# Matmuls that read their moving operand by turns from its two halves, in an attention and MLP kernel

## The chip, the cores and the metric

The kernel runs on one core of a Trainium2 chip. The metric is the device time of one launch in microseconds (us), the median of several runs. Work on the host before and after the launch is not in it.

## The reference

```python
scores = scale * np.matmul(z, z.transpose(0, 2, 1))   # scale = 1 / S
attn = np.maximum(scores, 0.0) ** 2
out = np.matmul(attn, v)
x = (u * out).reshape(B * S, D)
...
h = x @ w_in
relu6 = np.clip(h + 3.0, 0.0, 6.0)
g = h * relu6 / 6.0
return (g @ w_out).astype(np.float32)
```

B = 4 batches, S = 3008 tokens, D = 256, 64 columns of z, and 2048 columns between the two projections. Everything is float32, w_in and w_out come as float64.

## The kernel before, in words

Tokens stand along the free dimension of the tiles. Each batch is cut into six chunks of query tokens, five of 512 columns and one of 448 (`width`, L508), and into twelve pairs of key blocks of 128. A matmul takes a stationary operand of 128x128 and streams a moving operand of up to 512 columns into a PSUM bank. All of them go through one helper, `mm` (L74), so every matmul of the profile has line 75, and they are told apart by their tiles.

To keep precision, a float32 number is split into a high and a low part of type float32r, and a product is made of three: high by high, high by low, low by high.

- `scores` (L416) makes a pair of score blocks with two matmuls for each block (tile s, from zx and zy); ScalarE applies relu, ScalarE and VectorE square, and the result is split into ah and al. Part of the score blocks is not computed: they are the transposes of blocks made before, which come back from DRAM (`keep` L340, `fetch_pair` L325, `turn` L366).
- `av` (L513) sums attention times v into o: per chunk, pair and half of D six matmuls, four with ah as the moving operand (against vl and vh) and two with al; the last pair of a chunk has five. `first_av` (L496) is the same for the very first pair.
- `times_u` (L544) multiplies o by u, which `load_u` (L537) brought in as a block of two chunks, and `split_x` (L552) cuts the block of 1024 or 960 tokens into a left and a right half of 512 or 480 columns, forms the sums of the second operand of a seven-product scheme for 2x2 blocks, and splits them into xh and xl.
- `group` (L671) makes for one block and one eighth of the 2048 columns the seven products, three matmuls each (tile m; `product`, L684), and the gate; results are split into gh and gl.
- `downs_of` (L607) has the second projection (tile y): six matmuls for each half of the tokens and of D, in `one` (L634) and, for the last eighth of the last block, `last_one` (L611). `store_y` (L651) scales y and writes it out.

The order of all this is written out by hand in the loop of L845: pair by pair, the score matmuls of the pair after next, the attention sums of this pair, and from pair 33 on pieces of `group` and `down` between them; the instructions run in that order on each engine. The program has 688 score matmuls, 3408 of attention, 2016 of the first projection, 2304 of the second, and ten on zeros at the start (`warm_up`, L818).

Of the kernel before, what the change touches and what calls it, by code (L numbers as in the profile page):

```python
# [13 lines left out]
B, S, D, DQK, DFF = 4, 3008, 256, 64, 2048  # L14
NT = B * S
P = 128
CH = 512
NCH = 6
# [4 lines left out]
NFP = NF // 2  # L23
# [18 lines left out]
def relu2_attention_then_hswish_mlp(  # L42
# [30 lines left out]

    def mm(out, lhsT, rhs, start, stop, part=False):  # L74
        nc.tensor.matmul(out, lhsT=lhsT, rhs=rhs, start=start, stop=stop, skip_group_check=part)  # L75

    def sub(out, a, b):
        nc.vector.tensor_tensor(out=out, in0=a, in1=b, op=ALU.subtract)  # L78
# [4 lines left out]
    def split(hi, lo, raw, rounded=False):  # L83
        if not rounded:
            nc.scalar.copy(out=hi, in_=raw)  # L85
        sub(lo, raw, f(hi))
# [409 lines left out]
    def first_av():  # L496

        for d in range(2):
            ot[d] = ps.tile([P, CH], F32, tag=f"o{d}", name=f"o{d}")
        ah, al = at[0, 0, 0]  # L500
        vh, vl = vt[0, 0]
        for k, (a, w, r) in enumerate(
            [(ah, w, r) for r in range(2) for w in (vl, vh)] + [(al, vh, r) for r in range(2)]
        ):
            for d in range(2):
                mm(ot[d], w[:, r, d * P:(d + 1) * P], a[:, r], k == 0, False)

    def width(c):  # L508
        return CH if c < NCH - 1 else S - CH * (NCH - 1)

    ot = {}

    def av(b, c, p, d):  # L513

        n = width(c)
        first = p == pairs_of(b, c)[0]
        if first:
            home = f"y0{d}" if (b, c) == (0, 1) else f"o{d}"
            ot[d] = ps.tile([P, CH], F32, tag=home, name=f"o{d}")
        o = ot[d][:, :n]  # L520
        ah, al = at[b, c, p]
        vh, vl = vt[b, p]
        dd = slice(d * P, d * P + P)
        last = p == NPAIR - 1
        passes = [(w, ah, r) for r in range(2) for w in (vl, vh)]
        passes += [(vh, al, r) for r in range(1 if last else 2)]
        for k, (w, a, r) in enumerate(passes):
            mm(o, w[:, r, dd], a[:, r, :n], first and k == 0, last and k == len(passes) - 1)

    raw_x = {}  # L530

    def tokens(i):

        b, c = divmod(i, NCH // 2)
        return b * S + 2 * c * CH, width(2 * c) + width(2 * c + 1)
# [14 lines left out]
    xt = {}  # L550
# [56 lines left out]
    def downs_of(i, q, gs):  # L607

        n = tokens(i)[1] // 2

        def last_one(h, e):  # L611
            o = yt_t[h, e]
            gh, gl = gs[h]
            ee = slice(e * P, e * P + P)
            w = wo[i, q]
            y = rpool.tile([P, 2, CH], F32, tag="r", name="y")[:, e, :n]
            order = (1, 0) if h else (0, 1)
            for r in order:
                mm(o[:, :n], w[:, 1, r, ee], gh[:, r, :n], False, False)
                mm(o[:, :n], w[:, 0, r, ee], gh[:, r, :n], False, False)  # L620
                mm(o[:, :n], w[:, 0, r, ee], gl[:, r, :n], False, r == order[1])
            if e:
                nc.vector.tensor_scalar(
                    out=y, in0=o[:, :n], scalar1=1.0 / 6.0, scalar2=None, op0=ALU.mult
                )
            else:
                nc.scalar.activation(out=y, in_=o[:, :n], func=AF.Copy, scale=1.0 / 6.0)
            t0 = tokens(i)[0] + h * n
            nc.sync.dma_start(out=yt[e * P:(e + 1) * P, t0:t0 + n], in_=y)

        if (i, q) == (NPR - 1, NFP - 1):
            return [(h, e, last_one) for h in range(2) for e in range(2)]

        def one(h, e):  # L634
            if q == 0:
                yt_t[h, e] = ps.tile([P, CH], F32, tag=f"y{h}{e}", name=f"y{h}{e}")
            o = yt_t[h, e][:, :n]
            gh, gl = gs[h]
            ee = slice(e * P, e * P + P)
            w = wo[i, q]  # L640
            for r in range(2):
                mm(o, w[:, 1, r, ee], gh[:, r, :n], q == 0 and r == 0, False)
                mm(o, w[:, 0, r, ee], gh[:, r, :n], False, False)
            for r in range(2):
                mm(o, w[:, 0, r, ee], gl[:, r, :n], False, q == NFP - 1 and r == 1)
            if q == NFP - 1 and e == 1:
                store_y(i, h)

        return [(h, e, one) for h in range(2) for e in range(2)]
# [21 lines left out]
    def group(m, x_bank="x", y_bank="y"):  # L671


        i, q = divmod(m, NFP)
        n = tokens(i)[1] // 2
        if m + 1 < NPR * NFP:
            wi[m + 1] = fetch_w("in", (m + 1) % NFP)
        wo[i, q] = fetch_w("out", q)
        w = wi.pop(m)

        def bank(tag):
            return ps.tile([P, CH], F32, tag=tag, name="m")[:, :n]

        def product(o, a, b, start, stop):  # L684
            xh, xl = xt[i][b]
            mm(o, w[:, 1, a], xh, start, False, True)
            mm(o, w[:, 0, a], xl, False, False, True)
            mm(o, w[:, 0, a], xh, False, stop, True)

        def temp(name):  # L690
            return rpool.tile([P, 2, CH], F32, tag="r", name=name)[:, :, :n]

        def gate(out, h):
            nc.vector.scalar_tensor_tensor(  # L694
                out=out, in0=out, scalar=6.0, in1=h, op0=ALU.min, op1=ALU.mult
            )

        def g_tiles(h):
            gh = gpool.tile([P, 2, CH], F32R, tag=f"gh{h}", name=f"gh{h}")
            gl = gpool.tile([P, 2, CH], F32R, tag=f"gl{h}", name=f"gl{h}")  # L700
            return gh[:, :, :n], gl[:, :, :n]

        end = m == NPR * NFP - 1

        def by_halves(g, r, t):
            split(g[0][:, r], g[1][:, r], t[:, r])

        c21 = bank(x_bank)
        product(c21, A11, B11, True, False)
        ra = temp("ra")  # L710
        nc.scalar.copy(out=ra[:, 1], in_=c21)
        yield
        y = bank(y_bank)
        product(y, A12, B21, True, True)
        add(ra[:, 1], ra[:, 1], y)
        yield
        product(c21, S2, T2, False, False)
        hb = temp("hb") if x_bank == "o0" else hpool.tile([P, 2, CH], F32, tag="hb", name="hb")[:, :, :n]
        nc.scalar.copy(out=hb[:, 0], in_=c21)
        nc.scalar.activation(out=ra[:, 0], in_=ra[:, 1], func=AF.Relu, bias=three)  # L720
        late.append(lambda: gate(ra[:, 0], ra[:, 1]))
        yield
        product(c21, S3, T3, False, False)
        nc.scalar.copy(out=hb[:, 1], in_=c21)
        yield
        y = bank(y_bank)
        product(y, S1, T1, True, False)
        add(hb[:, 1], hb[:, 1], y)
        if end:
            ga, gb, rb = g_tiles(0), g_tiles(1), temp("rb")  # L730
            by_halves(ga, 0, ra)
            nc.scalar.activation(out=rb[:, 1], in_=hb[:, 1], func=AF.Relu, bias=three)
        yield
        product(c21, A22, T4, False, True)
        nc.scalar.activation(out=ra[:, 1], in_=c21, func=AF.Relu, bias=three)  # L735
        gate(ra[:, 1], c21)
        yield
        product(y, S4, B22, False, True)
        add(hb[:, 0], hb[:, 0], y)
        if end:  # L740
            nc.scalar.copy(out=ga[0][:, 1], in_=ra[:, 1])
            nc.scalar.activation(out=rb[:, 0], in_=hb[:, 0], func=AF.Relu, bias=three)
            sub(ga[1][:, 1], ra[:, 1], f(ga[0][:, 1]))
            gate(rb[:, 1], hb[:, 1])
            yield
            nc.scalar.copy(out=gb[0][:, 1], in_=rb[:, 1])
            gate(rb[:, 0], hb[:, 0])
            sub(gb[1][:, 1], rb[:, 1], f(gb[0][:, 1]))
            by_halves(gb, 0, rb)
            downs.extend(downs_of(i, q, (ga, gb)))  # L750
            yield
            return
        ga = g_tiles(0)
        nc.scalar.copy(out=ga[0], in_=ra)  # L754
        yield
        sub(ga[1], ra, f(ga[0]))
        rb = temp("rb")
        nc.scalar.activation(out=rb, in_=hb, func=AF.Relu, bias=three)
        yield
        gate(rb, hb)  # L760
        gb = []

        def rest():
            gb.extend(g_tiles(1))
            split(*gb, rb)

        late.append(rest)
        downs.extend(downs_of(i, q, (ga, gb)))
        yield
# [56 lines left out]
    with tc.manual_schedule():  # L826
# [152 lines left out]
        last = (NPR - 1) * NFP - 1  # L979
# [31 lines left out]
_INS = ["zz", "v", "ut", "w_in", "w_out"]  # L1011


# [30 lines left out]
```

## Time and profile before

| | |
|---|---|
| median of 3 runs | 1907.8 us (1907.55 to 1912.01) |
| profiled execution, span | 1906.0 us |
| around the span (median less span) | 1.8 us |
| PE busy | 1892.2 us, 99%, 8426 matmuls |
| PE weight loads busy | 1574.6 us, 83%, 8426 |
| DVE busy | 1510.6 us, 79%, 1783 instructions |
| ACT busy | 1199.6 us, 63%, 1640 instructions |
| DMA moved | 329.50 MB, mean 173 GB/s |

The profiled execution is known by its span, from the first to the last instruction of the core. PE is TensorE, PEld its weight loads (which overlap its matmuls), DVE VectorE, ACT ScalarE, SP the engine that issues most DMAs. Ends of matmuls are modelled, so that neighbours overlap in the rows; the starts tell their pace.

### The profile page before, as it was taken

The page shows a single profiled execution, that of the slowest core. Times are in us where ns is not written, and L with a number is a line of the kernel's source. Part 1 is how long each engine was busy: PE and PEld are TensorE (multiplying, and loading weights), DVE is VectorE, ACT ScalarE, POOL GpSimd, SP SyncE. Part 2 cuts the span into 40 slices and gives each one's busy share as a digit, 9 for nine tenths or more (in the row PEclk, how much of TensorE's full clock was granted, in tenths as well). Part 3 has the DMA queues.
Part 4 walks back from the last instruction along what each step waited for, and adds up shares of the span by engine and source line. Part 5 has one row for each costly group of instructions (what it writes and reads, how often), then busy time and mean ns, then how long its engine had stood idle before and what let it go on. Part 6 is the DMA issues. An engine that isn't in the chain of part 4 may idle for free.

```text
span 1906.0 us, 23339 instructions
## 1 busy us (share of the span) xinstructions
PE 1892.2 (99%) x8426; PEld 1574.6 (83%) x8426; DVE 1510.6 (79%) x1783; ACT 1199.6 (63%) x1640; POOL 55.5 (3%) x90
## 2 busy tenths in 40 slices
PE   9999999999999999999999999999999999999999
PEld 7877788888888888888888888888888888888887
DVE  8899988878678778887767877888876786787766
ACT  7896656766556556576655655667665565564565
POOL 1000000100000000010000000001000000000000
PEclk9999999999999999999999999999999999999999
DMA  8878978665645675955655666595555567576343
GB/s 232 220 230 219 256 185 219 155 186 184 173 130 163 152 168 120 246 161 174 190 147 138 178 165 162 136 236 156 148 188 137 167 175 171 132 165 161 110 157 121
DMA packets 440307, 329.50 MB, mean 173 GB/s; under 512 B 278656, under 2 KB 397440, under 8 KB 440192
## 3 DMA queue, kind: packets, MB, share of 16 engines
q1 hardware_dynamic: 432672, 304.16, 59.1%
q0 software_dynamic: 7520, 23.86, 4.4%
q8 instruction: 66, 1.08, 0.2%
q14 instruction: 49, 0.40, 0.1%
HBM read 241.70 MB, written 86.25 MB: 172 GB/s over the span
## 4 chain that ended last, share of the span: by engine, by line
PE 66%; issue 23%; DVE 6%; ACT 2%; DMA 2%; SPq 0%; POOL 0%; DVEq 0%; POOLq 0%; ACTq 0%
PE o L75 26%; PE y L75 19%; PE m L75 16%; PE s L75 5%; DVE al L78 1%; DMA l<-d 1%; DVE gl L78 1%; DVE rb L694 0%; DMA dwout<-wh 0%; DVE r L452 0%; DVE rm L373 0%; DMA zraw<-in_zz_dram 0%; DVE xl L78 0%; SPq L334 0%; DVE vl L78 0%
## 5 line engine op out<-in xcount | busy, mean ns | idle before, releaser
L75 PE MATMUL m<-xh,wi 128*128 128x512 f32 (+1 forms) x1344 | 488.6, 387 | 2.8 <-DVE hb L81 1.2
L75 PE MATMUL o<-ah,vl 128*128 128x512 f32 (+1 forms) x1152 | 445.4, 387 | 2.4 <-DVE vl L78 1.2
L75 PE MATMUL o<-ah,vh 128*128 128x512 f32 (+1 forms) x1152 | 444.4, 386 | 0.0
L75 PE MATMUL y<-gh,wo 128*128 128x512 f32 (+1 forms) x1536 | 407.0, 386 | 1.2 <-DMA wo<-dwout 0.7
L75 PE MATMUL o<-al,vh 128*128 128x512 f32 (+1 forms) x1104 | 339.8, 386 | 0.5 <-DVE al L78 0.5
L75 PEld LDWEIGHTS y<-gh,wo 128*128 128x128 f32 x1536 | 288.0, 188 | 57.2 <-ACT gh L754 1.9
L75 PEld LDWEIGHTS m<-xh,wi 128*128 128x128 f32 x1344 | 252.2, 188 | 56.8 <-DVE hb L81 3.6
L75 PE MATMUL m<-xl,wi 128*128 128x512 f32 (+1 forms) x672 | 259.5, 386 | 0.0
L75 PEld LDWEIGHTS o<-ah,vl 128*128 128x128 f32 x1152 | 216.1, 188 | 48.2 <-DVE u L548 3.2
L75 PEld LDWEIGHTS o<-ah,vh 128*128 128x128 f32 x1152 | 216.4, 188 | 42.0
L75 PEld LDWEIGHTS o<-al,vh 128*128 128x128 f32 x1104 | 207.2, 188 | 40.4 <-DVE al L78 0.9
L433 ACT ACTIVATE rt<-s 128x512 f32<-128x512 f32 (+1 forms) x310 | 180.2, 595 | 90.2 <-PE s L75 84.3
L75 PE MATMUL y<-gl,wo 128*128 128x512 f32 (+1 forms) x768 | 234.7, 386 | 0.1
L452 DVE TENSOR_TENSOR r<-rt 128x1024 f32<-128x1024 f32 (+2 forms) x128 | 147.7, 1154 | 99.3 <-ACT rt L433 99.1
L81 DVE TENSOR_TENSOR hb<-hb,m 128x512 f32<-128x512 f32 (+1 forms) x192 | 129.0, 672 | 83.9 <-PE m L75 75.6
L735 ACT ACTIVATE ra<-m,three 128x512 f32<-128x512 f32 (+1 forms) x96 | 65.3, 681 | 198.9 <-PE m L75 195.4
L78 DVE TENSOR_TENSOR al<-r,ah 128x1024 fp32r<-128x1024 f32 (+3 forms) x147 | 164.6, 1120 | 7.1 <-ACT r L450 5.2
L75 PEld LDWEIGHTS y<-gl,wo 128*128 128x128 f32 x768 | 143.9, 188 | 28.5 <-DVE gl L78 0.9
L459 ACT ACTIVATE ah<-rt 128x1024 fp32r<-128x1024 f32 (+1 forms) x155 | 163.8, 1057 | 4.9
L78 DVE TENSOR_TENSOR gl<-rb,gh 128x1024 fp32r<-128x1024 f32 (+2 forms) x97 | 115.4, 1190 | 63.8 <-ACT gh L85 63.2
L78 DVE TENSOR_TENSOR al<-rm,ah 128x1024 fp32r<-128x1024 f32 (+1 forms) x132 | 155.4, 1177 | 1.3 <-ACT ah L400 0.9
L373 DVE STREAM_TRANSPOSE rm<-l 128x1024 f32<-128x1024 f32 (+2 forms) x132 | 149.6, 1133 | 4.1 <-DMA l<-d 4.1
(87 smaller groups left out, 2178.1 us busy)
## 6 DMA issues: line engine op xcount, KB each, us to landing
wi<-dwin SPq DMA_DIRECT2D x96, 896.0 KB, 5.4
d<-r SPq DMA_DIRECT2D x212, 256.0 KB, 3.2
wo<-dwout SPq DMA_DIRECT2D x96, 512.0 KB, 6.1
l<-d SPq DMA_DIRECT2D x304, 128.0 KB, 3.8
l<-d SPq DMA_DIRECT2D x160, 112.0 KB, 4.9
vraw<-in_v_dram POOLq DMA_DIRECT2D x33, 256.0 KB, 3.4
u<-in_ut_dram SPq DMA_DIRECT2D x8, 1024.0 KB, 5.3
out_dram<-y SPq DMA_DIRECT2D x16, 512.0 KB, 5.3
```

Of the source, the lines that this page charges most:

```text
L75: nc.tensor.matmul(out, lhsT=lhsT, rhs=rhs, start=start, stop=stop, skip_group_check=part)
L78: nc.vector.tensor_tensor(out=out, in0=a, in1=b, op=ALU.subtract)
L81: nc.vector.tensor_tensor(out=out, in0=a, in1=b, op=ALU.add)
L373: nc.vector.transpose(out=rn[:, :, :n].rearrange("p r (k e) -> p r k e", e=32), in_=t[:, :n // 32].rearrange("p k (r e) -> p r k e", r=2),)
L433: nc.scalar.activation(out=rn[:, r], in_=s[:, :n], func=AF.Relu, scale=1.0 / S)
L452: nc.vector.tensor_tensor(out=to, in0=of, in1=of, op=ALU.mult)
L459: nc.scalar.activation(out=hn, in_=rn, func=AF.Square)
L735: nc.scalar.activation(out=ra[:, 1], in_=c21, func=AF.Relu, bias=three)
```

## The change

A new helper `paired` gives a moving operand of n columns as a pattern in which the column index runs through two halves by turns: 0, n/2, 1, n/2 + 1, ... The moving operands of `av`, `first_av`, `group` and `downs_of` are read through it; those of `scores` and `warm_up` are not. A matmul's output is still written side by side, so the tokens of o, m and y stand in another order than those of the operand read. There are three such steps between the scores and the result (o, m and y), so the host lays the columns of u in the order of o before the launch, and puts the rows of the result back after it, out of all three orders (`of_y` applies `_paired` twice to each half of a block in u's order). The list of instructions on each engine, with their tiles and waits, is the same in both programs; of the 8426 matmuls 7728 have another pattern: 5720 of 512 columns, 1440 of 480 and 568 of 448. In a tile the two halves lie 2048/2 = 1024, 960 or 896 bytes apart in each partition.

```diff
@@ mm
+    def paired(ap):
+
+        return ap.rearrange("p (h n) -> p n h", h=2)
@@ first_av
-                mm(ot[d], w[:, r, d * P:(d + 1) * P], a[:, r], k == 0, False)
+                mm(ot[d], w[:, r, d * P:(d + 1) * P], paired(a[:, r]), k == 0, False)
@@ av
-            mm(o, w[:, r, dd], a[:, r, :n], first and k == 0, last and k == len(passes) - 1)
+            mm(o, w[:, r, dd], paired(a[:, r, :n]), first and k == 0, last and k == len(passes) - 1)
@@ downs_of, last_one
-                mm(o[:, :n], w[:, 1, r, ee], gh[:, r, :n], False, False)
-                mm(o[:, :n], w[:, 0, r, ee], gh[:, r, :n], False, False)
-                mm(o[:, :n], w[:, 0, r, ee], gl[:, r, :n], False, r == order[1])
+                mm(o[:, :n], w[:, 1, r, ee], paired(gh[:, r, :n]), False, False)
+                mm(o[:, :n], w[:, 0, r, ee], paired(gh[:, r, :n]), False, False)
+                mm(o[:, :n], w[:, 0, r, ee], paired(gl[:, r, :n]), False, r == order[1])
@@ downs_of, one
-                mm(o, w[:, 1, r, ee], gh[:, r, :n], q == 0 and r == 0, False)
-                mm(o, w[:, 0, r, ee], gh[:, r, :n], False, False)
+                mm(o, w[:, 1, r, ee], paired(gh[:, r, :n]), q == 0 and r == 0, False)
+                mm(o, w[:, 0, r, ee], paired(gh[:, r, :n]), False, False)
...
-                mm(o, w[:, 0, r, ee], gl[:, r, :n], False, q == NFP - 1 and r == 1)
+                mm(o, w[:, 0, r, ee], paired(gl[:, r, :n]), False, q == NFP - 1 and r == 1)
@@ group, product
-            xh, xl = xt[i][b]
+            xh, xl = (paired(x) for x in xt[i][b])
@@ host
+def _paired(a):
+
+    return a.reshape(2, -1).T.reshape(-1)
...
+    of_u = _np.concatenate([
+        b * S + c * CH + _paired(_np.arange(w)) for b in range(B) for c, w in enumerate(widths)
+    ])
+    of_y = _np.concatenate([
+        _paired(_paired(half))
...
-        "ut": u.reshape(NT, D).T,
+        "ut": u.reshape(NT, D)[of_u].T,
...
-    return _np.ascontiguousarray(r.results[0]["out_0_dram"].T)
+    y = _np.empty((NT, D), _np.float32)
+    y[of_y] = r.results[0]["out_0_dram"].T
+    return y
```

## Rows read from the trace of the kernel before

**Rows 1.** The page: span, busy time of each engine, granted clock in 40 slices.

```profile
span 1906.0 us, 23339 instructions
...
PE 1892.2 (99%) x8426; PEld 1574.6 (83%) x8426; DVE 1510.6 (79%) x1783; ACT 1199.6 (63%) x1640; POOL 55.5 (3%) x90
...
PEclk9999999999999999999999999999999999999999
```

**Rows 2.** The page: chain that ended last, shares of the span by engine.

```profile
PE 66%; issue 23%; DVE 6%; ACT 2%; DMA 2%; SPq 0%; POOL 0%; DVEq 0%; POOLq 0%; ACTq 0%
```

**Rows 3.** The page: groups of changed matmuls; busy us, mean ns, idle before.

```profile
L75 PE MATMUL m<-xh,wi 128*128 128x512 f32 (+1 forms) x1344 | 488.6, 387 | 2.8 <-DVE hb L81 1.2
...
L75 PE MATMUL o<-ah,vl 128*128 128x512 f32 (+1 forms) x1152 | 445.4, 387 | 2.4 <-DVE vl L78 1.2
...
L75 PE MATMUL o<-ah,vh 128*128 128x512 f32 (+1 forms) x1152 | 444.4, 386 | 0.0
...
L75 PE MATMUL y<-gh,wo 128*128 128x512 f32 (+1 forms) x1536 | 407.0, 386 | 1.2 <-DMA wo<-dwout 0.7
...
L75 PE MATMUL o<-al,vh 128*128 128x512 f32 (+1 forms) x1104 | 339.8, 386 | 0.5 <-DVE al L78 0.5
...
L75 PE MATMUL m<-xl,wi 128*128 128x512 f32 (+1 forms) x672 | 259.5, 386 | 0.0
...
L75 PE MATMUL y<-gl,wo 128*128 128x512 f32 (+1 forms) x768 | 234.7, 386 | 0.1
```

**Rows 4.** Timeline, weight loads (start us, us): the warm-up, and one after it.

```profile
2.05 0.33 PEld L75 LDWEIGHTS warm<-warm 128*128 128x128 f32 x1
...
3.33 0.33 PEld L75 LDWEIGHTS warm<-warm 128*128 128x128 f32 x1
...
6.31 0.19 PEld L75 LDWEIGHTS s<-zy,zx 128*128 128x128 f32 x1
```

**Rows 5.** Timeline of PE, 900 to 905 us: eleven matmuls of 512 columns.

```profile
900.45 0.39 PE L75 MATMUL s<-zy,zx 128*128 128x512 f32 x1
...
902.94 0.39 PE L75 MATMUL s<-zy,zx 128*128 128x512 f32 x1
```

**Rows 6.** Timeline of PE, 910.8 to 911.4 us: four matmuls of 256 columns.

```profile
910.88 0.28 PE L75 MATMUL s<-zy,zx 128*128 128x256 f32 x1
...
911.35 0.40 PE L75 MATMUL o<-ah,vl 128*128 128x512 f32 x1
```

**Rows 7.** Timeline of PE, 999.1 to 1001.6 us: eleven matmuls of 480 columns.

```profile
999.14 0.38 PE L75 MATMUL m<-xl,wi 128*128 128x480 f32 x1
...
1001.53 0.39 PE L75 MATMUL s<-zy,zx 128*128 128x512 f32 x1
```

**Rows 8.** Timeline of PE, 776.2 to 777.5 us: six matmuls of 448 columns.

```profile
776.26 0.36 PE L75 MATMUL o<-ah,vl 128*128 128x448 f32 x1
...
777.48 0.40 PE L75 MATMUL m<-xh,wi 128*128 128x512 f32 x1
```

**Rows 9.** Busy time of each engine by stretches.

```profile
core 0: us, PE busy (x) PEld busy (x) DVE busy (x) ACT busy (x) POOL busy (x), PEclk, DMA share, GB/s
50.00:100.00 50.00, 50.00 (x223) 41.40 (x222) 44.14 (x71) 43.17 (x59) 2.85 (x4) 1.00 0.86 221
100.00:150.00 50.00, 47.91 (x206) 37.62 (x205) 48.96 (x78) 45.27 (x64) 2.85 (x4) 1.00 0.76 237
150.00:200.00 50.00, 49.32 (x215) 39.67 (x214) 48.37 (x74) 31.92 (x45) 2.86 (x4) 1.00 0.81 217
200.00:250.00 50.00, 47.96 (x208) 38.44 (x207) 44.46 (x68) 31.20 (x43) 2.14 (x3) 1.00 0.88 234
1200.00:1400.00 200.00, 199.85 (x899) 167.73 (x899) 167.60 (x194) 132.23 (x184) 10.80 (x17) 1.00 0.65 175
1400.00:1600.00 200.00, 200.00 (x897) 167.31 (x896) 147.54 (x160) 118.91 (x162) 0.00 (x0) 1.00 0.58 158
```

More of the change, by code (lines that the diff above doesn't have):

```diff
@@ L1011, with _orders @@
 _INS = ["zz", "v", "ut", "w_in", "w_out"]
+def _paired(a):
+    return a.reshape(2, -1).T.reshape(-1)
+def _orders():
+    import numpy as _np
+    widths = [CH] * (NCH - 1) + [S - CH * (NCH - 1)]
+    of_u = _np.concatenate([
[3 more added lines that the diff above has]
+        _paired(_paired(half))
+        for b in range(B)
+        for c in range(0, NCH, 2)
+        for half in of_u[b * S + c * CH:b * S + c * CH + widths[c] + widths[c + 1]].reshape(2, -1)
+    ])
+    return of_u, of_y
 def kernel(**inputs):
@@ L1021 @@
     u, v, z = (_np.asarray(inputs[k]) for k in "uvz")
+    of_u, of_y = _orders()
     zt = z.transpose(0, 2, 1)
```

## The prediction

> **What bounds the kernel now.** I read the page first: TensorE (PE) is busy for 99% of the span at full granted clock, VectorE (DVE) for 79% and ScalarE (ACT) for 63% [rows 1]. Since a busy PE row contains modelled ends, I then looked at the chain of waits: 66% of the span is PE's own work and 23% is issue, that is, time in which PE waited for nothing that the profile shows; DVE, ACT and DMA together hold 10% [rows 2]. So the kernel ends when PE has got through its list of 8426 matmuls [rows 1], and the question is what one of them costs from start to start. The mean duration of a group does not tell that (386 to 387 ns for nearly every group, because neighbours overlap [rows 3]); the timeline does, by dividing a stretch without a wait by the matmuls in it.
>
> - 512 columns: from 900.45 to 902.94 us eleven matmuls start, 226.4 ns each [rows 5].
> - 480 columns: from 999.14 to 1001.53 us eleven start, 217.3 ns each [rows 7].
> - 448 columns: from 776.26 to 777.48 us six start, 203.3 ns each [rows 8].
> - 256 columns: from 910.88 to 911.35 us four start, 117.5 ns each [rows 6].
>
> In the warm-up, weight loads start every (3.33 - 2.05) / 3 = 0.427 us, with 512 columns streamed behind each [rows 4]. That is 0.833 ns a column, 1.2 columns per ns: the lower of the two clock levels (the clock column does not show it there, but a load takes 0.33 us against 0.19 us later), with nothing lost beside the columns. At the upper level the same columns should take half, 0.4167 ns each: 213.3, 200.0, 186.7 and 106.7 ns. **PE thus loses 13.1 ns per matmul of 512 columns, 17.3 of 480, 16.6 of 448 and 10.8 of 256, and loses it at the upper level alone.** The array takes its columns without a gap when they are wanted half as fast, so I look for the loss in what feeds it.
>
> **The change, part by part.** On no engine does an instruction move, come or go, and no wait changes; tiles, weights, destinations and DMAs stay. What changes is the order in which 7728 matmuls read their moving operand: columns 0, n/2, 1, n/2 + 1 and so on, instead of 0, 1, 2. The groups give the counts: attention 1152 + 1152 + 1104 = 3408, projection in 1344 + 672 = 2016, projection out 1536 + 768 = 2304 [rows 3]. By width, with the loops of the code: attention has 142 matmuls in each of 24 chunks, 20 of them 512 wide and 4 of them 448 (2840 and 568); the projections have 12 token blocks, 8 of them 512 wide and 4 of them 480 (2880 and 1440). So 5720 of 512 columns, 1440 of 480 and 568 of 448, together 3,874,304 columns. The 688 score matmuls and the 10 of the warm-up stay as they are. The reordering of u and of the result is done outside the launch, at nothing: on the chip u lands, is multiplied by the attention sum and is split in the same tiles and by the same instructions, whatever token stands in a column.
>
> What these matmuls cost now: 5720 x 226.4 + 1440 x 217.3 + 568 x 203.3 = 1295.0 + 312.9 + 115.5 = 1723.4 us, or 0.4448 ns a column.
>
> No row of this trace shows a strided moving operand, so the new price is bounded from both sides. **Lower bound:** half the warm-up's price [rows 4], 0.4167 ns a column, 3,874,304 x 0.4167 = 1614.4 us, a gain of 109.0 us. Less I exclude: no row shows more than one column per tick of either level. **Upper bound:** the warm-up's full price, one column per tick of the lower clock, 0.8333 ns: 3228.6 us, a loss of 1505 us. I take a value at the lower end for the likeliest case. The reason is where the loss stands: it is absent when the same kind of operand is read at half the rate [rows 4], so it comes from a source that can't quite deliver one unbroken row at the upper rate. Two separate places, each asked for at half the upper rate, are then in the position of the warm-up rows, which lose nothing. That is an inference from rows; that two places are served side by side is not shown.
>
> The Trainium skill speaks against this change: "Advanced Engine Details and Errata", section "Memory Cachelines", says that SBUF is read in lines of 16 bytes, that at least two hits on a line are needed to absorb the access latency, and that a different line at each access pays a penalty. Reading by turns hits a different line every time, so by that page alone the sum would be a loss towards the upper bound; no run here shows it yet. By the page "TensorE: Matmul & The Clock Gate", section "Wait — 56ns, not 53.3ns?", about 2.5 ns remain per matmul at the upper level; the sum would then be 7728 x 2.5 = 19 us smaller, 1830 instead of 1811.
>
> What hides behind PE: the gain is had only where the other engines keep up. From 50 to 250 us DVE is busy for 44.14 + 48.96 + 48.37 + 44.46 = 185.9 of 200 us and PE already idles 4.8 us [rows 9]. A PE that is 5.7% faster (109.0 / 1906) would want that stretch in 188.6 us, DVE at 98.6%; I let the first 250 us yield half of their 14 us, so 7 are lost. Later DVE holds 167.6 of 200 us from 1200 to 1400 and 147.5 from 1400 to 1600, with PE idle for 0.15 and 0.0 us [rows 9]; shortened, that is 89% and 78%. Between the 0.15 us at 84% and the 4.8 us at 93% I take 5 us for all later stretches. What is late next is thus DVE, in its answers to PE's products (hb, ra) and in the low parts al and gl. Sum: -109.0 + 7 + 5 = -97 us. The span is 1906.0 us and the median of the runs 1907.8; the 1.8 us around the span stay. **1907.8 - 97 = 1811 us.**
>
> **The rivals.**
>
> 1. *Part of the loss belongs to the matmul, not to its columns.* Between 256 and 512 columns the price rises by (226.4 - 117.5) / 256 = 0.4254 ns a column [rows 5, 6]; only 0.0087 ns of that is above 0.4167, and some 8.5 ns are left per matmul, whatever its width. If reading by turns takes away the part by column alone, the gain is 3,874,304 x 0.0087 = 34 us, and since DVE then has room I take nothing off: 1874 us. For it: the 10.8 ns at 256. Against: 480 and 448 columns lose more than 512, so the loss is no straight line in the width, and four matmuls are few.
>
> 2. *The loss has nothing to do with the order of reading.* Each of these matmuls comes with its own weight load (8426 of either [rows 1]); if the loss is the exchange of the weights, 7728 patterns change and nothing else: 1908 us, 1902 to 1913. For it: the loss has the size of some fixed step (10.8 to 17.3 ns over widths that differ by a factor of two). Against: in the warm-up a weight load goes with each matmul as well and costs nothing [rows 4].
>
> 3. *The change makes it slower: the reader holds one place at a time.* If two neighbouring columns are fetched together when they lie side by side, and separately when they lie half an operand apart, then each column costs a fetch of its own. The place is the moving read of all 7728 matmuls; the price is up to the warm-up's 0.8333 ns a column, 1907.8 + 1505 = 3413 us, PE alone bounding everything and DVE and ACT idling. It decides from 0.4448 ns a column upwards; each 0.01 ns above that is 39 us. For it: no moving operand in the trace before is read in any way but side by side, so nothing excludes it, and the loss at the upper level shows that the reading has no room to spare. Against: nothing in the rows beyond the inference above. The Trainium skill's rule on lines is this rival.
>
> **How the numbers follow.** The full gain gets 0.45, the part by column 0.18, no effect 0.15 and the slower case 0.22. Faster by over 0.3% (the least that a measurement of this kernel can tell from no change, some 6 us) is 0.45 + 0.18 = 0.63, within it 0.15, slower 0.22. The likeliest case's own range is 1793 to 1865: downwards the whole 109 us with 6 us for the reading of the paces, upwards half of that gain kept back. The full range takes in rivals 1 and 2 and the mild end of rival 3, up to 0.456 ns a column (1907.8 + 42 = 1950 us), for which I count 0.04 of its 0.22: 1793 to 1950 leaves out some 0.18.
>
> **What would show it.** In the changed kernel's timeline, dense rows of the attention and of both projections should start every 213 to 216 ns at 512 columns and every 200 to 203 at 480, while the score matmuls, which still read side by side, keep about 226: they are the control within the same trace. The number of matmuls, the granted clock and the durations on DVE and ACT should stay; DVE's share should rise to about 83% (1510.6 / 1811), and PE should idle more between 50 and 250 us. Paces of 226 throughout would show rival 2; some 222 at 512 columns rival 1; anything above 227 in the changed groups with the scores unchanged is rival 3, and then DVE and ACT shares fall. I am wrong if the changed groups run faster and the span does not follow: then DVE was nearer to being the bound than its 79% says.

## The result, and the profile after

The changed kernel takes **1847.3 us** (median of 4 runs, 1844.13 to 1848.44), the kernel before 1907.9 us beside it: a ratio of 0.9677, with a 95% interval of 0.9664 to 0.9691. It is 60.6 us faster; 97 were forecast. The profiled execution took 1846.6 us, with a span of 1844.8, against 1906.0 before [rows 1]. That makes 61.2 us to account for.

The page of the changed kernel, with the busy times, the chain of waits by engine and the first two groups of changed matmuls:

```profile
span 1844.8 us, 23339 instructions
...
PE 1810.3 (98%) x8426; PEld 1583.5 (86%) x8426; DVE 1516.7 (82%) x1783; ACT 1196.9 (65%) x1640; POOL 55.5 (3%) x90
...
PE 55%; issue 24%; DVE 12%; ACT 4%; DMA 3%; SPq 1%; POOL 0%; DVEq 0%; ACTq 0%; POOLq 0%
...
L75 PE MATMUL m<-xh,wi 128*128 128x512 f32 (+1 forms) x1344 | 476.3, 378 | 10.5 <-DVE hb L85 5.9
L75 PE MATMUL o<-ah,vl 128*128 128x512 f32 (+1 forms) x1152 | 432.6, 376 | 9.8 <-DVE u L552 7.1
```

The numbers of instructions are those of before. DVE's share of the chain has doubled, from 6% [rows 2] to 12%, and the idle time ahead of these two groups has grown from 2.8 and 2.4 us [rows 3] to 10.5 and 9.8. The mean durations (387 to 378 and 376) again say little; the pace stands in the timeline (start us, duration us). Two scores and, behind them, a dense run of changed matmuls of 512 columns:

```profile
745.25 0.40 PE L75 MATMUL s<-zy,zx 128*128 128x512 f32 x1
...
745.72 0.38 PE L75 MATMUL o<-ah,vl 128*128 128x512 f32 x1
...
749.60 0.38 PE L75 MATMUL o<-ah,vl 128*128 128x512 f32 x1
...
980.56 0.97 PE L75 MATMUL y<-gh,wo 128*128 128x480 f32 x4
...
981.78 0.37 PE L75 MATMUL m<-xh,wi 128*128 128x480 f32 x1
...
763.95 0.35 PE L75 MATMUL o<-ah,vh 128*128 128x448 f32 x1
...
764.89 0.38 PE L75 MATMUL m<-xh,wi 128*128 128x512 f32 x1
```

From 745.72 to 749.60 us eighteen matmuls of 512 columns start, 215.6 ns each (226.4 before [rows 5]). From 980.56 to 981.78 six of 480 start, 203.3 ns each (217.3 [rows 7]); from 763.95 to 764.89 five of 448, 188 ns each (203.3 [rows 8]). The two scores, whose reading is as before, take 0.47 us together, 235 ns each. Over the whole trace, the median time from one start to the next is 216, 203 and 189 ns in the changed groups, all 0.42 ns a column, and for the scores it went from 227 to 233 ns.

Busy time and matmuls by stretches, of the changed kernel (the columns are those of [rows 9]):

```profile
50.00:100.00 50.00, 49.86 (x228) 42.24 (x226) 46.79 (x70) 44.22 (x61) 2.85 (x4) 1.00 0.88 226
100.00:150.00 50.00, 44.12 (x190) 34.91 (x191) 49.20 (x76) 43.27 (x61) 2.85 (x4) 1.00 0.72 234
150.00:200.00 50.00, 46.07 (x207) 38.28 (x207) 49.24 (x69) 30.74 (x44) 2.86 (x4) 1.00 0.74 203
200.00:250.00 50.00, 46.20 (x205) 38.85 (x204) 48.80 (x74) 30.25 (x43) 1.43 (x2) 0.98 0.86 234
400.00:800.00 400.00, 398.20 (x1870) 350.98 (x1869) 323.57 (x357) 251.99 (x339) 5.94 (x9) 1.00 0.66 176
800.00:1200.00 400.00, 398.89 (x1870) 350.95 (x1869) 322.14 (x356) 255.98 (x347) 8.15 (x13) 1.00 0.61 165
1200.00:1600.00 400.00, 397.81 (x1872) 351.45 (x1871) 322.70 (x361) 257.43 (x353) 10.80 (x17) 1.00 0.67 177
```

And of the kernel before, the same view of the last three stretches:

```profile
400.00:800.00 400.00, 400.00 (x1789) 333.76 (x1788) 309.35 (x339) 239.83 (x322) 3.25 (x5) 1.00 0.63 166
800.00:1200.00 400.00, 399.43 (x1787) 333.57 (x1786) 306.63 (x339) 245.74 (x335) 10.83 (x17) 1.00 0.60 165
1200.00:1600.00 400.00, 399.85 (x1794) 335.04 (x1794) 315.14 (x353) 251.14 (x345) 10.80 (x17) 1.00 0.61 166
```

From 400 to 1600 us the rows count 5612 matmuls of PE instead of 5370, 4.5% more (one that runs across an edge counts on both sides). From 50 to 250 us they count 228 + 190 + 207 + 205 = 830, where it had been 852 [rows 9]: that stage did not get faster but slower, with DVE busy for 194.0 of 200 us (185.9 before). What PE waited for up to 310 us, the two largest waits (us in total, times, longest):

```profile
PE m L75 <- DVE hb L85: 3.7, 3, 2.1
PE o L75 <- DVE al L82: 2.7, 3, 1.3
```

DVE itself had grown slower. The kernel makes its float32 weights out of float64 in seven DVE steps per piece, in which every second word is read or written (a step of 8 bytes). One of them, before and after (busy us, mean ns):

```profile
L152 DVE SCALAR_TENSOR_TENSOR wraw<-wraw 128x512 f32<-128x512 uint32 x16 | 11.0, 688 | 0.3
```

```profile
L156 DVE SCALAR_TENSOR_TENSOR wraw<-wraw 128x512 f32<-128x512 uint32 x16 | 14.0, 876 | 0.3
```

All seven groups together went from 64.2 to 76.7 us. No instruction of DVE was changed.

**Where the time went.** Pace: 10.8 x 5720 + 14.0 x 1440 + 15.3 x 568 = 61.8 + 20.2 + 8.7 = 91 us. Scores: 592 of 512 columns, 6 ns slower each, -3.5 us. That leaves 26 us that did not arrive. Both programs have the same list of matmuls, so each can be set beside itself in the other trace. The 1254 that start in the first 300 us of the kernel before take 3.0 us longer in the changed one, where the pace, less the scores, would have gained 10.5: 13.5 us are missing. Those from 300 to 400 us lack 3.4 us, those from 400 to 1600 us 3.2 (they gain 52.3 of 55.5), those behind 5.7. Waits are most of it: up to 310 us PE's grew from 8.5 to 18.6 us, behind that from 1.1 to 11.6. The largest behind 310 us are those of the attention for u: 5.9 of the 7.1 us that the page shows above.

### The profile page after: what moved, and what is told of

Same layout as the page of the kernel before. It is cut to its first block, busy times and chain, and to the rows that moved or that the text cites. A ratio compares the mean times of both kernels' runs of the same rounds, so it can differ in the third digit from the quotient of the medians.

```text
span 1844.8 us, 23339 instructions
## 1 busy us (share of the span) xinstructions
PE 1810.3 (98%) x8426; PEld 1583.5 (86%) x8426; DVE 1516.7 (82%) x1783; ACT 1196.9 (65%) x1640; POOL 55.5 (3%) x90
## 4 chain that ended last, share of the span: by engine, by line
PE 55%; issue 24%; DVE 12%; ACT 4%; DMA 3%; SPq 1%; POOL 0%; DVEq 0%; ACTq 0%; POOLq 0%
PE o L75 21%; PE y L75 15%; PE m L75 14%; PE s L75 5%; DVE al L82 2%; DMA l<-d 1%; DVE gl L82 1%; DVE rm L377 1%; DVE rb L698 1%; DMA zraw<-in_zz_dram 1%; ACT gh L758 1%; SPq L338 1%; DVE r L456 1%; DVE ra L698 1%; DVE xl L82 1%
## 5 line engine op out<-in xcount | busy, mean ns | idle before, releaser
L75 PE MATMUL m<-xh,wi 128*128 128x512 f32 (+1 forms) x1344 | 476.3, 378 | 10.5 <-DVE hb L85 5.9
L75 PE MATMUL o<-ah,vl 128*128 128x512 f32 (+1 forms) x1152 | 432.6, 376 | 9.8 <-DVE u L552 7.1
L75 PE MATMUL o<-ah,vh 128*128 128x512 f32 (+1 forms) x1152 | 431.7, 375 | 0.0
L75 PE MATMUL y<-gh,wo 128*128 128x512 f32 (+1 forms) x1536 | 388.7, 375 | 1.0 <-ACT gh L758 0.8
L75 PE MATMUL o<-al,vh 128*128 128x512 f32 (+1 forms) x1104 | 328.7, 376 | 2.9 <-DVE al L82 2.7
L75 PEld LDWEIGHTS m<-xh,wi 128*128 128x128 f32 x1344 | 254.5, 189 | 50.5 <-DVE hb L85 10.5
L75 PEld LDWEIGHTS o<-ah,vl 128*128 128x128 f32 x1152 | 217.3, 189 | 46.6 <-DVE u L552 9.6
L75 PE MATMUL m<-xl,wi 128*128 128x512 f32 (+1 forms) x672 | 252.4, 376 | 0.0
L75 PE MATMUL y<-gl,wo 128*128 128x512 f32 (+1 forms) x768 | 226.6, 376 | 1.0 <-DVE gl L82 0.5
```

## The experiments

In all but the weight-step run, the VectorE runs, the run with the scores and the far and close pair, `paired` is replaced by three patterns, `paired_a` in the attention, `paired_m` in the first projection and `paired_y` in the second, so that one run tries three orders. Paces are medians from start to start over the whole trace, at 512 columns unless said otherwise; ns. The times of these runs, and of the weight-step run, are of one execution each.

**How far apart the two places are.**

```diff
+    def paired_a(ap):
+        return ap.rearrange("p (g h n) -> p g n h", h=2, n=4)
+    def paired_m(ap):
+        return ap.rearrange("p (g h n) -> p g n h", h=2, n=16)
+    def paired_y(ap):
+        return ap.rearrange("p (g h n) -> p g n h", h=2, g=4)
```

> The changed kernel, but the two places read by turns lie closer: 16 bytes apart for the attention sums, 64 bytes for the first projection, 256 bytes (240 or 224 for narrower operands) for the second. Columns land in another order, so the result's rows are not the reference's. Theory A (two places are served side by side when they are far apart; the loss is that of one place asked twice in a row): attention stays at about 227 ns per 512 columns, the second projection is at 216, the first between; the span lies between 1850 and 1900 us. Theory B (the loss comes from the moving read and the weight load sweeping through the memory at the same pace, and any broken sweep removes it): all three at 216, span about 1845 us. Theory C (each change of a 16-byte line costs, whatever the distance): no difference between the three, all at the 216 of the changed kernel or all worse.

1843.5 us. With the places 16 bytes apart (attention), 64 bytes (first projection) or 240 to 256 (second), every group runs at 216, 203 and 189 ns. Six matmuls of the attention, 16 bytes apart, in 1.30 us:

```profile
746.43 0.38 PE L75 MATMUL o<-ah,vl 128*128 128x512 f32 x1
...
747.73 0.38 PE L75 MATMUL m<-xh,wi 128*128 128x512 f32 x1
```

So the halves need not be far apart. In the form put to this run, that places far apart are served side by side, the prediction's reason falls; 16 bytes apart are still two places, and the runs below take up the rest of it.

**Steps instead of turns.**

```diff
+    def paired_a(ap):
+        return ap.rearrange("p (n h) -> p h n", h=2)
+    def paired_m(ap):
+        return ap.rearrange("p (n h) -> p h n", h=4)
+    def paired_y(ap):
+        return ap.rearrange("p (n h) -> p h n", h=16)
```

> The changed kernel, but each operand is read with a step instead of by turns from two halves: step of 2 columns (8 bytes) for the attention sums, 4 (16 bytes) for the first projection, 16 (64 bytes) for the second, in as many passes. The result's rows are in another order. Theory A: neighbours in time lie 8, 16 and 64 bytes apart, close together, so the loss of 11 ns stays in attention (227 per 512 columns) and may stay in the others. Theory B: the weights are still swept at their pace and the moving read runs faster through the memory, so the loss is gone or smaller in all three (216 to 220). Theory C: 227 with the step of 8 bytes, where two columns share a line of 16 bytes, and towards 427 with steps of 16 and 64 bytes, where none do: span of 2500 us or more.

3566.9 us. Steps of 8, 16 and 64 bytes take 451, 461 and 434 ns. Two matmuls of the attention, one of 480 columns of the first projection, four of the second:

```profile
1701.05 0.63 PE L75 MATMUL o<-ah,vh 128*128 128x512 f32 x1
1701.50 0.63 PE L75 MATMUL o<-ah,vl 128*128 128x512 f32 x1
...
1703.31 0.61 PE L75 MATMUL m<-xh,wi 128*128 128x480 f32 x1
1703.75 0.61 PE L75 MATMUL m<-xl,wi 128*128 128x480 f32 x1
...
1709.08 1.91 PE L75 MATMUL y<-gh,wo 128*128 128x512 f32 x4
1710.81 0.61 PE L75 MATMUL y<-gl,wo 128*128 128x512 f32 x1
```

The starts are 0.45 us apart in the attention, 0.44 at 480 columns, and 1.73 / 4 = 0.43 in the second projection. A price such as the prediction's slower rival had thus exists: this is 0.85 to 0.90 ns a column, at its upper bound and a little above. Turns between two places do not pay it. By the Trainium skill, "Advanced Engine Details and Errata", section "Memory Cachelines", two accesses to one line of 16 bytes are enough, and another line at each access is penalised. The runs differ on both points: a step of 8 bytes has two columns in each 16 bytes and takes 451 ns, and turns change the place at each column and take 216.

**More places by turns.**

```diff
+    def paired_a(ap):
+        return ap.rearrange("p (h n) -> p n h", h=4)
+    def paired_m(ap):
+        return ap.rearrange("p (h n) -> p n h", h=16)
+    def paired_y(ap):
+        return ap.rearrange("p (h n w) -> p n h w", h=2, w=2)
```

> The changed kernel with other turns: four places (a quarter apart) for the attention sums, sixteen places for the first projection, two halves but two neighbouring columns from each in turn for the second. The result's rows are in another order. Theory A: 216 per 512 columns with four and with sixteen places; with two neighbouring columns from each, 227 if a pair side by side is what loses, 216 if the change of place every few columns is enough. Theory B: 216 in all three. Theory C: four and sixteen places touch a new line with every column and the same line again only after four or sixteen, so if lines that are open matter, sixteen places are slower than two: above 300 ns; two neighbours from each, 216.

2702.4 us. Four places take 283 ns, sixteen 433, and two neighbours of one half followed by two of the other 333. Attention and, at 480 columns, sixteen places:

```profile
1301.19 0.45 PE L75 MATMUL o<-ah,vl 128*128 128x512 f32 x1
...
1301.76 0.73 PE L75 MATMUL o<-al,vh 128*128 128x512 f32 x2
...
1302.72 0.58 PE L75 MATMUL m<-xl,wi 128*128 128x480 f32 x1
1303.13 0.58 PE L75 MATMUL m<-xh,wi 128*128 128x480 f32 x1
```

Two matmuls of the attention take 0.57 us, one of 480 columns with sixteen places 0.41. Of the orders so far, turns are good with two places and one column from each; the three of this run are worse than side by side. Four places are each asked at a quarter of the rate and lose 283 - 213 = 70 ns, so being asked more slowly is not what helps.

**A stepped weight load, on the kernel before.** The moving operands stay side by side; the stationary ones of the attention are read with a step of 8 bytes, those of the second projection with one of 16.

```diff
...
-            mm(o, w[:, r, dd], a[:, r, :n], first and k == 0, last and k == len(passes) - 1)
+            mm(o, w[:, r, d::2], a[:, r, :n], first and k == 0, last and k == len(passes) - 1)
...
-            w = wo[i, q]
+            w = wo[i, q].rearrange("p k r d -> p k (r d)")
+            w = [[w[:, k, 2 * e + r::4] for r in range(2)] for k in range(2)]
...
```

> The kernel before (moving operands side by side), but the stationary operand is loaded with a step: every second column of v (8 bytes) for the attention sums, every fourth (16 bytes) of w_out for the second projection; the first projection is unchanged and is the control. Other columns of v and w_out take part, so the result is another one. Theory A (the loss belongs to the moving read alone): attention and second projection stay at 227 ns per 512 columns, span 1905 to 1915 us. Theory B (moving read and weight load collide because both sweep side by side): the pace of attention and of the second projection changes, down to 216 or up, by at least 3 ns, while the first projection stays at 227; span outside 1895 to 1920 us.

1948.1 us. Time and paces are those of theory B, in its slower direction; only the control did not hold still. The weight loads themselves grow (busy us, mean ns):

```profile
L75 PEld LDWEIGHTS y<-gh,wo 128*128 128x128 f32 x1536 | 389.1, 313 | 14.9 <-ACT gh L754 1.1
L75 PEld LDWEIGHTS m<-xh,wi 128*128 128x128 f32 x1344 | 253.1, 188 | 50.5 <-DVE hb L81 2.2 <-ACT rt L433 1.9 <-DVE ra L81 1.1
L75 PEld LDWEIGHTS o<-ah,vl 128*128 128x128 f32 x1152 | 224.1, 195 | 41.1 <-DVE vl L78 1.8 <-DVE u L548 1.7 <-ACT ah L492 0.8
```

Side by side a load takes 188 ns, with 8 bytes' step 195, with 16 bytes' 313; the pace goes from 227 to 233 in the attention and in the second projection (at 480 columns, from 216 to 237), and even the unchanged first projection stands at 230. The run shows that the pace depends on how the weights are read as well, by what way it does not show. Why the side-by-side row loses its 11 ns it does not decide either.

**Less work for VectorE, on both kernels.** The seven steps that make float32 of float64 become one.

```diff
-        f0, f1 = f(t0), f(top)
+        f0 = f(t0)
...
-            out=t0, in0=top, scalar1=0x07FFFFFF, scalar2=3,
-            op0=ALU.bitwise_and, op1=ALU.logical_shift_left,
+            out=t0, in0=top, scalar1=0x7FFFFFFF, scalar2=None, op0=ALU.bitwise_and
```

The other six steps are left out.

> The kernel before, with VectorE relieved in the first 300 us: of the seven steps that turn a float64 weight into a float32 one, one is left (the upper word taken as it is), so the weights are others and the result too; 96 instructions of some 0.7 us, about 65 us of VectorE, are gone. Theory D1 (in the first 300 us VectorE sets the pace of both kernels): PE's waits of that stretch, some 14 us, go for the most part: 1893 to 1900 us. Rival D2 (those waits are round trips through DRAM or ScalarE): 1904 to 1910 us.

> The changed kernel with the same steps left out (other weights, another result). Theory D1 (what the faster matmuls could have gained in the first 300 us was lost to VectorE): 1812 to 1825 us, so that the distance to the kernel before relieved in the same way grows from 61 to 72 to 82 us. Rival D2: the distance stays at 58 to 64 us, the time at 1840 to 1848.

The kernel before does not change: 1908.8 us, ratio 1.0005 (0.9996 to 1.0015). The changed one comes to 1838.1 us, ratio 0.9633 (0.9619 to 0.9648), 9 us below its 1847.3. The distance between the two grows from 61 to 70.7 us. Both forecasts of theory D1 failed; for the changed kernel the time and the distance lie between D1 and its rival. PE's waits up to 310 us in the kernel before had been 8.5 us, not 14, of which 4.9 were for DVE (the 1.5 at the very start aside); without the steps 2.4 are left, but those for ScalarE (rt) grew from 1.5 to 4.6 us. Ahead of the longest, 2.7 us, ScalarE itself stood waiting for a DMA before a copy of weights:

```profile
99.14 0.62 ACT L101 CAST wh<-t 128x512 fp32r<-128x512 f32 x1 [4.19 <-DMA dwin<-wh]
```

The changed kernel without the steps has the same wait, longer (5.25 us). So VectorE held back about 9 us of the gain in the first stages, net of that new wait.

**A model of the reading: two lanes.** By then one picture fitted the prices side by side, by turns and with a step, though not four places by turns (283) nor two neighbours from each half (333). In it, columns go by turns to two lanes; each lane fetches four neighbouring columns (16 bytes) at a time. Side by side, a lane uses two of the four; by turns from two places, all four; with a step, one.

```diff
+    def paired_a(ap):
+        return ap.rearrange("p (g h n) -> p g n h", h=2, n=2)
+    def paired_m(ap):
+        return ap.rearrange("p (h n f) -> p f n h", h=2, f=2)
+    def paired_y(ap):
+        return ap.rearrange("p (h n f) -> p f n h", h=2, f=4)
```

> The changed kernel with other orders: attention reads columns 0, 2, 1, 3 of each four (two places 8 bytes apart by turns); the first projection reads by turns from its two halves, but every second column, in two passes; the second projection likewise, every fourth column in four passes. The result's rows are in another order. Theory E (every second column of the stream goes to a lane of its own; a lane fetches a block of four neighbouring columns and pays when it needs a new block after fewer than four): in attention both lanes take two columns from a block, as when read side by side, 0.44 to 0.46 ns a column, 226 to 234 per 512; in the first projection also two, 226 to 234; in the second one, 0.85 to 0.90 ns, 430 to 461. Rival A (only two columns side by side one after the other lose): attention 216. Rival F (a step within a lane is what doubles the price, by whatever length): first projection above 400 as the second.

2411.3 us, with 227, 227 and 451 ns, where the model had all three. Five matmuls of 480 columns of the first projection, four of the second, four of 512 of the attention:

```profile
1150.70 0.37 PE L75 MATMUL m<-xh,wi 128*128 128x480 f32 x1
...
1151.76 0.38 PE L75 MATMUL m<-xh,wi 128*128 128x480 f32 x1
1151.97 1.86 PE L75 MATMUL y<-gh,wo 128*128 128x480 f32 x4
1153.66 1.03 PE L75 MATMUL y<-gl,wo 128*128 128x480 f32 x2
...
1154.99 0.39 PE L75 MATMUL o<-ah,vl 128*128 128x512 f32 x1
...
1155.90 0.61 PE L75 MATMUL o<-al,vh 128*128 128x512 f32 x2
```

1.06 / 5 = 212 ns, 1.69 / 4 = 423 ns and 0.91 / 4 = 228 ns. The first projection reads by turns from its halves here as in the changed kernel, but only every second column, so that a lane uses two of four: the gain is gone. Turns alone are not what helps, and neither is a half that is asked at half the rate, which each half is here too.

**Where the model ends.**

```diff
+    def paired_a(ap):
+        return ap.rearrange("p (h n w) -> p n h w", h=2, w=4)
+    def paired_m(ap):
+        return ap.rearrange("p (h n) -> p n h", h=8)
+    def paired_y(ap):
+        return ap.rearrange("p (g h n) -> p g n h", h=4, n=4)
```

> The changed kernel with three other orders, the result's rows in another order: attention reads four neighbours from one half, then four from the other; the first projection eight places by turns; the second four places by turns, 16 bytes apart. Theory E with one block in each lane: attention 226 to 234 ns per 512 columns (two columns of a block in a lane, then another block); the first projection as with sixteen places, 430 and above; the second 450 and above. Rival H (a lane keeps two blocks or more, and pays by how many it has to hold): attention 216; the first projection between the 283 ns of four places and the 433 of sixteen; the second 283 as four places far apart.

2564.5 us. Four neighbours from one half and then four from the other take 251 ns, eight places 490, four places 16 bytes apart 268; rows of the second projection (480 columns, 253 ns) and of the attention (253 ns):

```profile
1303.68 1.17 PE L75 MATMUL y<-gh,wo 128*128 128x480 f32 x4
1304.69 0.67 PE L75 MATMUL y<-gl,wo 128*128 128x480 f32 x2
...
1305.65 0.41 PE L75 MATMUL o<-ah,vl 128*128 128x512 f32 x1
...
1306.66 0.67 PE L75 MATMUL o<-al,vh 128*128 128x512 f32 x2
```

A lane that keeps one block should have taken 226 to 234, over 430 and over 450; one that keeps several, about 216, 283 to 433, and 283. Neither fits all three. What a lane keeps when it comes back to a block after others stays open.

**The scores too.** Their moving operands are read through `paired` as well.

```diff
-        zx, zy = (z[:, :n] for z in zt[b, c])
+        zx, zy = (paired(z[:, :n]) for z in zt[b, c])
```

> The changed kernel with the score matmuls read by turns too. The order of the columns of blocks computed and blocks transposed then differs, so the result is another; the work is the same. The 592 score matmuls of 512 columns go from 233 to 216 ns (10 us), the other 96 save 1 us: 1834 to 1840 us if PE's pace alone counts; the other groups stay at 216. Rival: the 233 ns of the scores in the changed kernel come from something else than their own order, and they stay above 225: 1844 to 1849 us.

1839.6 us (1838.3 to 1845.1), ratio 0.9649 (0.9634 to 0.9664), 7.7 us below the changed kernel (5.9 below its second measurement, the far run further down). Two scores now take 0.43 us instead of the 0.47 above:

```profile
745.01 0.38 PE L75 MATMUL s<-zy,zx 128*128 128x512 f32 x1
...
745.44 0.38 PE L75 MATMUL o<-ah,vl 128*128 128x512 f32 x1
```

The estimate from the paces is (233 - 216) x 592 = 10 us. To use it, the kernel would need z in a second order; that was not tried.

**Far against close places.** The changed kernel again (far, 896 to 1024 bytes), and one whose places are 64 bytes apart, with the host's order changed along.

```diff
     def paired(ap):
-        return ap.rearrange("p (h n) -> p n h", h=2)
+        return ap.rearrange("p (g h n) -> p g n h", h=2, n=16)
...
 def _paired(a):
-    return a.reshape(2, -1).T.reshape(-1)
+    return a.reshape(-1, 2, 16).transpose(0, 2, 1).reshape(-1)
```

> The changed kernel once more, beside the next one on the same chip: 1844 to 1849 us.

> The changed kernel with the two places 64 bytes apart in all 7728 matmuls, and the host's order of u and of the result to match, so that the result is the reference's. PE's pace does not depend on the distance (216 at 16 bytes, 64 bytes, 256 bytes and 1024 bytes). Theory G (far places disturb VectorE's steps with a stride of 8 bytes on the weights, which took 10.0 us more in the changed kernel and 1.8 us more with close places): VectorE gets back 7 to 10 us in the first 300 us, where PE waits for it, and the time falls by 3 to 9 us: 1836 to 1845 us, below the changed kernel in the same rounds by more than 0.15%. Rival (those steps were longer by chance of what ran beside them): the two differ by less than 0.15%.

Far: 1845.5 us, ratio 0.9673 (0.9660 to 0.9686). Close: **1838.05 us** (1836.05 to 1838.4), ratio 0.9633 (0.9619 to 0.9646), 7.4 us below far and the fastest kernel here. The DVE step shown above, far and close:

```profile
L156 DVE SCALAR_TENSOR_TENSOR wraw<-wraw 128x512 f32<-128x512 uint32 x16 | 14.1, 881 | 0.3
```

```profile
L156 DVE SCALAR_TENSOR_TENSOR wraw<-wraw 128x512 f32<-128x512 uint32 x16 | 11.0, 688 | 0.3
```

PE's pace is the same in both, and DVE's seven steps are back at what they were before the change; no other group of DVE or ScalarE differs by 0.5 us. Of the close kernel, two of the stretches in which DVE sets the pace:

```profile
100.00:150.00 50.00, 46.61 (x205) 37.55 (x204) 49.20 (x78) 44.24 (x61) 2.85 (x4) 1.00 0.77 235
150.00:200.00 50.00, 48.01 (x219) 40.64 (x218) 48.65 (x76) 32.02 (x45) 2.86 (x4) 1.00 0.82 226
```

424 matmuls instead of 397, with DVE as full as before: the stage still ends on DVE, but DVE gets more done.

The run with three distances shows in one trace which matmuls lengthen these steps. The same DVE step there (L161), beside the attention (16 bytes) and beside the second projection (256 bytes):

```profile
73.60 0.69 DVE L161 SCALAR_TENSOR_TENSOR wraw<-wraw 128x512 f32<-128x512 uint32 x1
...
178.14 0.96 DVE L161 SCALAR_TENSOR_TENSOR wraw<-wraw 128x512 f32<-128x512 uint32 x1
```

Of its sixteen, the three that run beside the second projection take 0.76 to 0.96 us, the thirteen others 0.64 to 0.70, beside the first projection (64 bytes) too. In the changed kernel thirteen of sixteen take 0.87 to 0.96 us; the other three, 0.64 to 0.75, run while PE waits or mostly beside scores, which it reads side by side.

## Why the prediction was right and wrong

- **What bounds the kernel, and the loss per matmul: right.** The pace of PE set the time, and the order of reading took most of the loss away. Most signs came as forecast: changed groups at 215.6 and 203.3 ns (213 to 216 and 200 to 203), equal instruction counts, DVE at 82% (83%), PE idle in the early stretches. Three did not hold: the scores as a control moved by 6 ns, DVE's durations grew, and the granted clock fell twice.
- **The floor: mis-sized by 18 us.** The lower bound of 0.4167 ns a column was taken as the price itself; a gain of 109.0 was booked and the rows give 91. At 512, 480 and 448 columns 2.3, 3.3 and 1.3 ns stay with each matmul in the dense rows. The prediction had the number at hand: the Trainium skill, "TensorE: Matmul & The Clock Gate", section "Wait — 56ns, not 53.3ns?", has about 2.5 ns left per matmul at the upper level, with which its estimate came to 1830 us; the trace agrees, with its 1.3 to 3.3 ns. The warm-up rows [rows 4], at the lower level, could not show it.
- **"I let the first 250 us yield half": wrong by 6.5 us.** To 300 us 13.5 us are missing, 7 were taken off. The prediction counted with DVE's work as it was, and the stage had DVE at 97% of its time with steps that had grown by 12.5 us. That DVE would be late next was right; that the change would slow DVE itself was not thought of. The close kernel, which takes that away alone, gets back 7.4 us.
- **Five us for later stages: 12 measured**, 3.2 of them from 400 to 1600 us. DVE was late there in hb and ra, as forecast, but most in u (5.9 us), which the prediction did not name.
- **The scores: -3.5 us, not counted.** They were to keep their pace.
- **Sum:** -109.0 + 18.3 + 13.5 + 12.3 + 3.5 = -61.4 us, beside 61.2 measured between the spans.
- **The reason given was wrong, though the number followed; that the price fell to the lower end was in this part luck.** By "two separate places, each asked for at half the upper rate", the two halves read with every second column (227 ns) and four places (283 ns) should have been as cheap as the change, and they are not. The distance, from 16 to 1024 bytes, is of no account. The picture of lanes fits the same columns at 0.42, 0.44 and 0.85 to 0.90 ns, but not all the orders tried; what the reading does stays open.
- **The rivals.** Part by matmul (222 ns expected) and no effect (226) fell with the 215.6 ns. The slower rival fell for this order, but a price such as it gave is real for steps: 0.85 to 0.90 ns a column against 0.8333.

## What to carry to other kernels

Where a dense run of float32r matmuls starts every 227 ns at 512 columns, read the moving operand by turns from two places, one column from each, every column used; a short distance (64 bytes here) is enough and leaves VectorE's stepped accesses alone, but 8 bytes are too short (227 ns). Avoid steps in the moving operand: 8, 16 and 64 bytes each doubled the price. And when one engine becomes faster, look in the trace after at the durations of the other engines' unchanged instructions too, not only at their waits.

## What was not expected of the hardware

- PE reading by turns from two places far apart made DVE instructions with a step of 8 bytes 28% longer (688 to 876 and 881 ns): beside matmuls whose places are 256 or 1024 bytes apart, not at 16 or 64. Distance alone does not do it: with four far places (283 ns a matmul) it was 689, with every second column of two far halves (227 ns) 688, but with four neighbours from each far half (251 ns) 823. By what way PE holds DVE up is not shown.
- Side-by-side scores among changed matmuls are slower than before (227 to 233 ns), and the unchanged first projection beside stepped weight loads too (230).
- The granted clock shows 0.98 from 200 to 250 us in the changed kernel, where it was 1.00 before [rows 9]. PE had waited 2.1 us for hb; behind that, from 247.77 to 250.76 us, seven matmuls of 512 columns start 0.427 us apart, the pace of the warm-up and of the lower level of 1.2 GHz. The same comes once more behind a wait of 1.9 us for u that ends at 1663.4 us. Each cost some 1.5 us of the 26 that did not arrive; the far run, the same kernel, shows the second alone.
